# Linear attention into a tanh-shrink MLP: reordering the opening of batch 0 and moving work of batches 1 and 2 to later slots

## The chip, the cores and the metric

The kernel runs on one NeuronCore of one Trainium2 chip. The metric is the time of one execution on the device in microseconds (us); the median of three runs of the kernel before is 284.67 us (284.21 to 284.73). The engines are named as the profile names them: PE (TensorE matmuls), PEld (its weight loads), DVE (VectorE), ACT (ScalarE), POOL (GpSimd) and SP (the sync engine, which here only issues DMAs). Each engine takes its instructions strictly in the order in which they stand; an instruction that waits holds up everything behind it on its engine.

## The reference, cut to what matters

```python
def phi(x): return np.where(x > 0, x, np.exp(x) - 1.0) + 1.0      # = min(exp(x), max(x,0)+1)
q_p, k_p = phi(q), phi(k)                     # 8 batches, 8 heads, 576 tokens, 64 wide
kv  = einsum('bhsd,bhse->bhde', k_p, v)       # 64 x 64 for each head
z   = sum(k_p, axis=2)
num = einsum('bhsd,bhde->bhse', q_p, kv)
den = einsum('bhsd,bhd->bhs', q_p, z)[..., None] + 1e-06
x   = (num / den) -> [4608 tokens, 512]       # batch after batch
h   = x @ w_in                                # 512 -> 2048, "layer 1"
out = (h - tanh(h)) @ w_out                   # 2048 -> 512, "layer 2"
```

All inputs and the output are float32 in DRAM; the kernel turns them into bf16 as they are loaded.

## The kernel before, in words

**Two streams in one program.** The MLP runs over nine chunks `c` of 512 tokens. The attention runs over eight batches of 576 tokens and writes `xT`, the transposed input of layer 1. Batch 0 is computed before the MLP starts (the opening). The work of later batches is laid between the MLP's matmuls by hand: `s1[fi]` is a list of actions to be issued after layer 1's output block `fi` (16 blocks of 128 features, four matmuls of 128x512 each), and `s2[s]` one after slot `s` of layer 2 (16 slots of four matmuls). In chunk `c` the two streams work on batch `c+1` (denominator, numerator, scaling) and `c+2` (phi, kv, loads). The scheduling is manual: what the text of the kernel lists is the order on each engine, and nothing reorders it.

**Attention of a batch.** `phi_pieces` gives three actions for a half `i` of the heads: the exponential (ACT, tile `e`), `max(x,0)+1` (DVE, tile `r`) and the minimum of both (DVE, tile `qp` or `kp`). `a_kv`, `kv_cols_mm` and `b0_kv` make kv, which is copied from PSUM into `kz`; next to it `kz` holds the masked z. `qT` is the transposed phi(q): by PE transposes and two copies for each half in batches 0 and 1 (`a_qT_pe`), by one DMA transpose issued on SP from batch 2 on (`a_qT_dma`). `a_den` makes the denominators in one bank of PSUM and takes the reciprocal on DVE (`rden`, 128x144). The reciprocals are then brought to the layout of the numerators: for batch 0 and 1 by PE matmuls with a selection matrix (`b0_spread`, `a_spread_pe`), for batch 2 by DMA (`a_spread`): four small writes to DRAM (`ds`) and, once they have landed, two broadcast reads of 576 KB each (`rdb`). The numerators of batch 2 are then multiplied by `rdb` on DVE (`num_scale`, L401, four instructions of 128x512).

**The opening** on PE: 18 idle matmuls (`spin`), transposes of q, then z, kv, denominator and numerator of half 0 and 1 of the heads (`b0_z`, `b0_kv`, `a_den`, `b0_num`), the spread, and layer 1 of chunk 0, whose first four blocks are computed in halves of 256 tokens (L686), so that each of the eight scaling instructions (`b0_scale`, L304) releases four matmuls. The numerators are copied from PSUM to the tile `ns` by ACT (`b0_evac`, L293).

**PSUM** is one tile of eight banks, `ps_all`. Layer 1 of chunk 1 and later uses banks 0 to 5 in turn (`fi % 6`), so block `fi` can start only when DVE has read block `fi - 6` (the subtraction `gT`, L437, one instruction for two blocks, after ACT's tanh, L436).

**Loads.** q, k and v of a batch come by three DMAs issued on POOL. `qraw` and `kraw` have one buffer each. The loads of batch 3 stand on POOL behind `gate`, a copy of one element of `qT` of batch 2: they are issued only after the DMA transpose of batch 2 has landed. On SP the order at this place is: the DMA transpose of batch 2, the eight stores of chunk 0's output (held back in the list `later`), the four `ds` and two `rdb` transfers of batch 2, the stores of chunk 1.

Of the kernel before, what the change touches and what calls it, by code (L numbers as in the profile page):

```python
# [18 lines left out]
def kernel(  # L19
# [130 lines left out]
    def new_qT(b):  # L150
        qT_t[b] = work.tile([128, 2, J, 2, 64], BF16, name="qT")
# [4 lines left out]
            out=qT_t[b].rearrange("p i j g t -> p (i j) (g t)"),  # L156
            in_=qp_t[b].rearrange("p i j h d -> p (i j h d)"))

    def a_qT_pe(b, i, banks, on=None):
        if i == 0:  # L160
            new_qT(b)
        for n in range(2):
            j0, j1 = ((0, 5), (5, 9))[n]
            ps = banks().bitcast(BF16).rearrange("p (j t) -> p j t", t=128)
            for j in range(j0, j1):
                nc.tensor.transpose(ps[:, j - j0, :], qp_t[b][:, i, j].rearrange("p h d -> p (h d)"), ident)  # L166
            src = ps[:, 0:j1 - j0, :]
            dst = qT_t[b][:, i, j0:j1].rearrange("p j g t -> p j (g t)")
            if (on or "AV")[n] == "A":
                nc.scalar.copy(dst, src)  # L170
            else:
                nc.vector.tensor_copy(dst, src)

    def quads():

# [88 lines left out]
                                 v_b[0][rs, h, i, j, :], start=(j == 0), stop=(j == J - 1))  # L264

    def b0_kz(i):
        (nc.scalar.copy if i else nc.vector.tensor_copy)(kz_t[0][:, :, i, 0:64], ps_all[:, 2 * i:2 * i + 2, 0:64])

    def num_mm(b, i, bank_of):

# [14 lines left out]
    def b0_num(i):  # L285

        b0 = 2 * i
        num_mm(0, i, lambda h: b0 + h)
# [39 lines left out]
    def a_den(b, bank, parts=range(4)):  # L328

        kz, qT = kz_t[b], qT_t[b]  # L330
        ps = ps_all[:, bank, 0:J * 16]
        for t in range(4) if b == 0 else ():
            nc.tensor.matmul(ps[32 * t:32 * t + 32], eps[:, 0:32], one[:, 0:J * 16], start=True, stop=False)
        for n, p in enumerate((0, 2, 1, 3)):
            if n in parts:
                for t in range(4):
                    nc.tensor.matmul(ps[32 * t:32 * t + 32], kz[:, p // 2, p % 2, 64:96],  # L337
                                     qT[:, p % 2, :, p // 2, 16 * t:16 * t + 16],
                                     start=(n == 0 and b > 0), stop=(n == NP - 1))
        if b > 0:  # L340
            den = rpool.tile([128, J * 16], F32, name="den")
            nc.vector.tensor_scalar(den, ps, 1e-6, None, ALU.add)
        else:
            den = ps
        rden = rpool.tile([128, J * 16], F32, name="rden")
        nc.vector.reciprocal(rden, den)
        rden_t[b] = rden

    def a_split(b):
# [86 lines left out]
        nc.scalar.activation(th, h, AF.Tanh)  # L436
        nc.vector.tensor_sub(gT[:, fi:fi + 2, :], h, th)  # L437

    def l1act(fi, h, gT):
        th = mpool.tile([128, 2, 512], F32, name="th")[:, 0, :]  # L440
        nc.scalar.activation(th, h, AF.Tanh)  # L441
        nc.vector.tensor_sub(gT[:, fi, :], h, th)  # L442

    def gate(qT):

# [91 lines left out]
    for f in (eq0, rq0, mq0, eq1, rq1, mq1):  # L537
        f()
    spin(18)
    a_qT_pe(0, 0, side, "AV")  # L540
    (ek0, rk0, mk0), (ek1, rk1, mk1) = (phi_pieces(0, k_t, kp_t, "kp", i, 2 * i) for i in range(2))
    for f in (ek0, rk0):
        f()
    spin(5)
    a_qT_pe(0, 1, side, "AV")
    for f in (*ek1, mk0, rk1):
        f()
    spin(6)
    b0_z(0)
    spin(3)  # L550
    for f in mk1:
        f()
    b0_zc(0)
    b0_kv(0)
    b0_z(1)
    b0_zc(1)
    b0_kz(0)
    a_den(0, 4)
    ns0 = new_ns(0)
    spread_rest(0)  # L560
    b0_num(0)
    b0_kv(1)
    b0_kz(1)
    b0_evac(0, ns0)
    b0_num(1)
    b0_evac(1, ns0)
    b0_spread((0, 2, 1, 3), 0)
    for x in range(2):
        for n, p in enumerate((0, 2, 1, 3)):
            b0_scale(p, ns0, n, 4 * x, 4 * x + 4)  # L570

    def prepare():

# [12 lines left out]
    for c in range(NC):  # L586
# [4 lines left out]
        if c == 0:  # L591
            sub = {}

            def spread1():
                a_spread_pe(1, range(NP))
                for p in range(NP):
                    a_scale(1, p, sub["ns"], p)

            def kv1():
                a_kv(1, 4)  # L600
                pss = rest_mm(0, 4, 256)
                a_kz(1, 4)
                scale_rest(0, pss)

            def num1():
                ns = sub["ns"] = new_ns(1)
                for i in (1, 0):
                    b0 = 4 + 2 * i
                    num_mm(1, i, lambda h: b0 + h)
                    nc.scalar.copy(ns[:, i::2, 0:8, :].rearrange("p a j t -> p a (j t)"), ps_all[:, b0:b0 + 2, :])  # L610

            s2[0].append(lambda: a_qphi(1, 0))
            s2[1].append(lambda: a_qphi(1, 1))
            s2[4].append(lambda: a_kphi(1, 0))
            s2[5].append(lambda: (a_qT_pe(1, 0, Banks([4, 5])), a_qT_pe(1, 1, Banks([6, 7])), a_kphi(1, 1),
                                  load_q(2), load_k(2), load_v(2)))
            s2[2].append(prepare)
            s2[8].append(kv1)
            s2[9].append(lambda: (a_den(1, 4), num1(), spread_rest(1), a_split(1)))
            s2[12].append(spread1)  # L620

            qs, ks = [], []

            def exp2(pieces, src, store, name, i):
                pieces.append(phi_pieces(2, src, store, name, i))
                pieces[i][0]()

            def rest2(f):
                f[1]()
                f[2]()  # L630

            def k2(i):
                ks.append(phi_pieces(2, k_t, kp_t, "kp", i))
                ks[i][1]()

            s2[11].append(lambda: exp2(qs, q_t, qp_t, "qp", 0))
            s2[13].append(lambda: (rest2(qs[0]), exp2(qs, q_t, qp_t, "qp", 1)))
            s2[15].append(lambda: (rest2(qs[1]), a_qT_dma(2), [f() for f in later], k2(0), k2(1)))
        elif n1 < B:
            if c == 1:  # L640
                def kv2():
                    kv_cols_mm(2, 6, 0)
                    pss = rest_mm(1, 6, 256)
                    kz_copy(2, 6, 0)
                    scale_rest(1, pss)

                s1[8].append(kv2)
            if n1 < QS:
                s1[12].append(lambda: (a_den(n1, 6), a_spread(n1)))
            else:  # L650
                if c == 2:
                    s1[2].append(lambda: (q_den(n1, 0, 0), q_den(n1, 0, 1)))
                e = 2 * (c == 2)
                s1[3 + e].append(lambda: q_den(n1, 1, 0))
                s1[5 + e].append(lambda: q_den(n1, 1, 1))
                s1[7 + e].append(lambda: q_scale(n1))
            m = 12 if c == 1 else 9
            s2[m].append(lambda: a_num(n1, n2 if n2 < B else 0))
            if n2 < B:
                s2[m + 2].append(lambda: (q_zb(n2, 4 if c == 1 else 7), q_prod(n2)))  # L660
                if c > 1:
                    s2[15].append(lambda: (q_den(n2, 0, 0), q_den(n2, 0, 1)))
        if c == 1:
            for i in range(2):
                s1[1 + 2 * i].append(lambda i=i: (ks[i][0](), ks[i][2]()))
            s1[0].append(lambda: (a_vp(2, 0, nc.gpsimd), a_vp(2, 1, nc.gpsimd),
                                  gate(qT_t[n1]), load_k(n2), load_q(n2), load_v(n2)))
        if c >= 1 and n2 < B:
            d = 2
# [8 lines left out]
        if c == 0:  # L678

            first = Banks([4, 5, 6, 7, 0, 1, 2, 3])  # L680
            hs = [ps_all[:, n, :] for n in range(4)]
            for x in range(2):
                xs = slice(256 * x, 256 * x + 256)
                for n, p in enumerate((0, 2, 1, 3)):
                    for fi in range(4):
                        nc.tensor.matmul(hs[fi][:, xs], w_in_sb[:, p, fi * 128:(fi + 1) * 128], xT[:, p, xs],  # L686
                                         start=(x == 0 and n == 0), stop=(x == 1 and n == 3))
            for fi in range(4):
                l1act(fi, hs[fi], gT)
        for fi in range(4 if c == 0 else 0, NF):  # L690
            h = first() if c == 0 else ps_all[:, fi % 6, :]
            if c == 2 and fi == 1:

                for two in (0, 2):
                    for f, o in ((0, ps_all[:, 0, :]), (1, h)):
                        for p in (two, two + 1):
                            l1mm(c, f, o, p, p)
            elif c != 2 or fi > 1:
                for p in range(NP):
                    l1mm(c, fi, h, p, p)  # L700
            if c == 0:
                l1act(fi, h, gT)
            elif fi % 2:
                n = fi % 6
                l1act2(fi - 1, ps_all[:, n - 1:n + 1, :], gT)
            for f in s1[fi]:
                f()
# [56 lines left out]
```

## Time and profile before

| what | value |
|---|---|
| median of three runs | 284.67 us (284.21 to 284.73) |
| the profiled execution's own time | 284.32 us |
| its span, first to last instruction | 282.6 us |
| PE busy | 277.0 us, 98% of the span |
| DVE busy | 176.1 us, 62% |
| ACT busy | 145.6 us, 52% |
| POOL busy | 77.5 us, 27% |
| granted TensorE clock | 1.00 |
| first matmul of layer 1, chunk 0 (L686) | 16.82 us after the span's start |
| layer 1 of chunk 1 starts (L430) | 48.57 us |
| layer 1 of chunk 2 starts (L430) | 79.06 us |

The page gives busy time by engine, the span in 40 slices, the DMA queues, the chain of work that ended last and the costliest groups of instructions. A row of the timeline reads: start, duration, engine, source line, operation, output tile `<-` input tiles, shapes, count, and in brackets how long the engine had sat idle before it and what ended that. Starts are microseconds from the span's start. Durations of rows with a count above one reach from the first start to the last end. Line numbers are those of the kernel before.

### The profile page before, as it was taken

To read this page: it belongs to the slowest core of one execution; us is meant where nothing else is said; L and a number is where in the kernel's file an instruction comes from. 1 tells how busy PE (TensorE), PEld (TensorE's weight loads), DVE (VectorE), ACT (ScalarE), POOL (GpSimd) and SP (SyncE) were. 2 spreads that over 40 slices of the span, in tenths; PEclk is the share of its full clock that TensorE was granted. 3 is DMA by queue.
4 is the path that set the end of the run, shared out by engine and by line. 5 is a ranking of instruction groups with operands and counts; after the bars stand their busy time and mean duration, and the time that the engine had idled before them with its cause. 6 is when DMAs were issued, how large, how long until landed. Compare 5 with 4: busy or idle time off the path is not lost.

```text
span 282.6 us, 5093 instructions
## 1 busy us (share of the span) xinstructions
PE 277.0 (98%) x2084; PEld 131.9 (47%) x2084; DVE 176.1 (62%) x283; ACT 145.6 (52%) x176; POOL 77.5 (27%) x69
## 2 busy tenths in 40 slices
PE   8989999999999999999999999999999999999995
PEld 3564454454444454445444444444444444444443
DVE  5859977984779773977397639764870167006600
ACT  3648647946346753566366735572651365126411
POOL 8653120430361526233614360506050000000000
PEclk9999999999999999999999999999999999999999
DMA  6999999899994399049903792252115210230032
GB/s 103 199 207 212 205 207 209 172 192 197 236 237 76 71 194 217 5 84 162 220 22 73 115 240 60 48 110 48 29 22 123 58 32 2 57 79 13 2 74 75
DMA packets 38743, 33.12 MB, mean 117 GB/s; under 512 B 16160, under 2 KB 34624, under 8 KB 38592
## 3 DMA queue, kind: packets, MB, share of 16 engines
q0 software_dynamic: 17504, 18.35, 40.1%
q1 hardware_dynamic: 21216, 14.45, 21.8%
q8 instruction: 16, 0.26, 0.3%
q14 instruction: 7, 0.06, 0.1%
HBM read 38.14 MB, written 9.46 MB: 168 GB/s over the span
## 4 chain that ended last, share of the span: by engine, by line
PE 90%; DMA 5%; POOL 1%; ACT 1%; issue 1%; SPq 0%; DVE 0%; DVEq 0%; POOLq 0%
PE ps_all L430 43%; PE ps_all L451 41%; DMA v<-in_v_dram 3%; DMA out_dram<-osb 3%; PE ps_all L184 2%; PE ps_all L273 2%; PE ps_all L686 1%; ACT osb L462 1%; SPq L475 0%; POOL kraw L89 0%; PE ps_all L337 0%; POOL qraw L89 0%; PE ps_all L300 0%; PE ps_all L166 0%; PE ps_all L263 0%
## 5 line engine op out<-in xcount | busy, mean ns | idle before, releaser
L451 PE MATMUL ps_all<-w_out_sb,gT 128*128 128x512 bf16 x560 | 124.6, 379 | 0.0
L430 PE MATMUL ps_all<-xT,w_in_sb 128*128 128x512 bf16 x560 | 122.7, 379 | 0.0
L437 DVE TENSOR_TENSOR gT<-ps_all,th 128x1024 bf16<-128x1024 f32 x64 | 77.8, 1218 | 46.4 <-ACT th L436 46.4
L436 ACT ACTIVATE th<-ps_all 128x1024 f32<-128x1024 f32 x64 | 65.5, 1024 | 46.9 <-PE ps_all L430 46.9
L430 PEld LDWEIGHTS <-w_in_sb 128*128 128x128 bf16 x560 | 54.6, 98 | 65.5
L451 PEld LDWEIGHTS <-gT 128*128 128x128 bf16 x560 | 53.8, 98 | 63.2 <-issue 0.2
L462 ACT COPY osb<-ps_all 128x512 f32<-128x512 f32 (+1 forms) x36 | 20.7, 582 | 56.4 <-PE ps_all L451 40.0
L245 POOL TENSOR_TENSOR qp<-qp,rd 128x1152 bf16<-128x1152 bf16 x10 | 21.0, 2118 | 39.1 <-issue 23.7
L231 POOL TENSOR_TENSOR pr<-qp,zb 128x1152 f32<-128x1152 bf16 x10 | 23.5, 2362 | 21.6 <-ACT zb L224 21.6
L236 DVE TENSOR_REDUCE dn<-pr 128x9 f32<-128x576 f32 x20 | 14.5, 745 | 12.2 <-POOL pr L231 12.2
L136 ACT ACTIVATE e<-qraw 128x1152 bf16<-128x1152 bf16 x16 | 18.5, 1161 | 5.4 <-DMA qraw<-in_q_dram 5.4
L136 ACT ACTIVATE e<-kraw 128x1152 bf16<-128x1152 bf16 x15 | 17.4, 1162 | 1.9 <-DMA kraw<-in_k_dram 1.9
L138 DVE TENSOR_TENSOR qp<-e,r 128x1152 bf16<-128x1152 bf16 x16 | 12.1, 759 | 4.4 <-ACT e L136 3.3
L92 POOL DMA_DIRECT2D kraw<-in_k_dram x7 | 5.4, 769 | 33.1 <-DVE r L137 17.7
L138 DVE TENSOR_TENSOR kp<-e,r 128x1152 bf16<-128x1152 bf16 x15 | 11.4, 763 | 4.4 <-ACT e L136 3.5
L441 ACT ACTIVATE th<-ps_all 128x512 f32<-128x512 f32 x16 | 9.4, 597 | 5.5 <-PE ps_all L686 3.7
L442 DVE TENSOR_TENSOR gT<-ps_all,th 128x512 bf16<-128x512 f32 x16 | 10.4, 687 | 2.7 <-ACT th L441 1.7
L532 PE MATMUL ps_all<-zero 128*128 128x512 bf16 x32 | 10.1, 475 | 1.2 <-DVE zero L485 1.2
L92 POOL DMA_DIRECT2D qraw<-in_q_dram x7 | 5.2, 741 | 16.7 <-ACT e L136 7.3
L137 DVE TENSOR_SCALAR r<-qraw 128x1152 bf16<-128x1152 bf16 x16 | 7.4, 465 | 0.4 <-DMA qraw<-in_q_dram 0.4
L460 DVE COPY osb<-ps_all 128x128 f32<-128x128 f32 x1 | 0.3, 292 | 11.6 <-DMA out_dram<-osb 11.6
L199 DVE COPY vp<-v 128x1152 bf16<-128x1152 bf16 x10 | 5.3, 525 | 3.2 <-DMA v<-in_v_dram 3.2
(105 smaller groups left out, 141.1 us busy)
## 6 DMA issues: line engine op xcount, KB each, us to landing
out_dram<-osb SPq DMA_DIRECT2D x62, 128.0 KB, 2.5
qraw<-in_q_dram POOLq DMA_DIRECT2D x7, 576.0 KB, 10.5
kraw<-in_k_dram POOLq DMA_DIRECT2D x7, 576.0 KB, 7.8
v<-in_v_dram POOLq DMA_DIRECT2D x6, 576.0 KB, 11.4
w_in_sb<-in_moe_w_in_dram POOLq DMA_DIRECT2D x3, 512.0 KB, 13.1
w_out_sb<-in_moe_w_out_dram POOLq DMA_DIRECT2D x3, 512.0 KB, 16.3
v<-in_v_dram POOLq DMA_DIRECT2D x4, 288.0 KB, 12.9
rdb<-ds SPq DMA_DIRECT2D x2, 576.0 KB
```

The source lines that it names most:

```text
L92: nc.gpsimd.dma_start(out=t.rearrange("q h i j d -> q (h i) (j d)"), in_=x.rearrange("(n q) x -> q n x", n=4))
L136: return (lambda: nc.scalar.activation(e, x, AF.Exp), lambda: nc.vector.tensor_scalar(r, x, 0.0, 1.0, ALU.max, ALU.add), lambda: nc.vector ...
L138: lambda: nc.vector.tensor_tensor(y, e, r, ALU.min))
L231: nc.gpsimd.tensor_mul(pr_t[b][:, i].rearrange("p j h d -> p j (h d)"), qp_t[b][:, i].rearrange("p j h d -> p j (h d)"), zb_t[b][:, i].uns ...
L236: nc.vector.tensor_reduce(dn_t[b][:, i, :, h], pr_t[b][:, i, :, h, :], mybir.AxisListType.X, ALU.add)
L245: nc.gpsimd.tensor_mul(x, x, rd[:, i].unsqueeze(2).to_broadcast([128, J * 2, D]))
L430: nc.tensor.matmul(h, w_in_sb[:, p, fi * 128:(fi + 1) * 128], xT[:, p, c * 512:(c + 1) * 512], start=(n == 0), stop=(n == NP - 1))
L436: nc.scalar.activation(th, h, AF.Tanh)
L437: nc.vector.tensor_sub(gT[:, fi:fi + 2, :], h, th)
L442: nc.vector.tensor_sub(gT[:, fi, :], h, th)
L451: nc.tensor.matmul(o, gT[:, fi, i * 128:(i + 1) * 128], w_out_sb[:, fi, :], start=(fi == 0), stop=(fi == NF - 1))
L462: nc.scalar.copy(osb[:, f0:f1], o[:, f0:f1])
```

## The change

In the opening:

- the copies of `qT` become actions that the caller places; the DVE copy of half 1 stays first, the ACT copy (`t1a`) goes behind the two exponentials of k's second half;
- one `spin` matmul less at two places (5 to 4, 3 to 2);
- `kz` of half 0 is copied by ACT and `kz` of half 1 by DVE (the reverse of before);
- the reciprocal of batch 0 is two instructions, over columns 0 to 127 and 128 to 143;
- on PE the spread stands ahead of the numerator of half 1 (before: behind it), and the evacuation of half 0 ahead of kv of half 1;
- the eight scalings go by halves of the heads first (pairs 0, 2 for all tokens, then pairs 1, 3), and the first 32 matmuls of layer 1 are reordered to match; the four PSUM outputs are laid across two banks each.

In batches 1 and 2:

- chunk 0's layer 2: kv of batch 1 from slot 8 to 9, denominator and numerator from 9 to 10, spread and scaling from 12 to 13, the exponential of q of batch 2 (half 0) from 11 to 13; the exponential of half 1 leaves slot 13;
- chunk 1's layer 1 takes its blocks 0 and 1 in an interleaved order, as chunk 2 did already;
- phi(q) half 1 of batch 2, the DMA transpose of batch 2 and the held-back stores go from slot 15 of chunk 0 to behind block 1 of chunk 1 (only `max(x,0)+1` of that half stays in slot 15); phi(k) of batch 2 from behind blocks 1 and 3 to behind 3 and 5; kv of batch 2 from behind block 8 to 10; denominator and spread of batch 2 from behind block 12 to 13; the gate and the loads of batch 3 from behind block 0 to 1.

```diff
-    def a_qT_pe(b, i, banks, on=None):
+    def a_qT_pe(b, i, banks, on="AV"):
...
-            if (on or "AV")[n] == "A":
-                nc.scalar.copy(dst, src)
-            else:
-                nc.vector.tensor_copy(dst, src)
+            copies.append((nc.scalar.copy if on[n] == "A" else nc.vector.tensor_copy, dst, src))
+        return [lambda f=f, d=d, x=x: f(d, x) for f, d, x in copies]
...
-        (nc.scalar.copy if i else nc.vector.tensor_copy)(kz_t[0][:, :, i, 0:64], ps_all[:, 2 * i:2 * i + 2, 0:64])
+        (nc.vector.tensor_copy if i else nc.scalar.copy)(kz_t[0][:, :, i, 0:64], ps_all[:, 2 * i:2 * i + 2, 0:64])
...
-        nc.vector.reciprocal(rden, den)
+        for x in (slice(0, 128), slice(128, 144)) if b == 0 else (slice(0, 144),):
+            nc.vector.reciprocal(rden[:, x], den[:, x])
...
-    a_qT_pe(0, 0, side, "AV")
+    for f in a_qT_pe(0, 0, side):
+        f()
...
-    spin(5)
-    a_qT_pe(0, 1, side, "AV")
-    for f in (*ek1, mk0, rk1):
+    spin(4)
+    t1a, t1v = a_qT_pe(0, 1, side)
+    for f in (t1v, *ek1, t1a, mk0, rk1, *mk1):
         f()
     spin(6)
     b0_z(0)
-    spin(3)
-    for f in mk1:
-        f()
+    spin(2)
     b0_zc(0)
     b0_kv(0)
+    b0_kz(0)
     b0_z(1)
     b0_zc(1)
-    b0_kz(0)
     a_den(0, 4)
     ns0 = new_ns(0)
-    spread_rest(0)
     b0_num(0)
+    b0_evac(0, ns0)
     b0_kv(1)
     b0_kz(1)
-    b0_evac(0, ns0)
+    spread_rest(0)
+    b0_spread((0, 2, 1, 3), 0)
     b0_num(1)
     b0_evac(1, ns0)
-    b0_spread((0, 2, 1, 3), 0)
-    for x in range(2):
-        for n, p in enumerate((0, 2, 1, 3)):
-            b0_scale(p, ns0, n, 4 * x, 4 * x + 4)
+    for i in range(2):
+        for x in range(2):
+            for n, p in ((2 * i, i), (2 * i + 1, 2 + i)):
+                b0_scale(p, ns0, n, 4 * x, 4 * x + 4)
...
-            s2[8].append(kv1)
-            s2[9].append(lambda: (a_den(1, 4), num1(), spread_rest(1), a_split(1)))
-            s2[12].append(spread1)
+            s2[9].append(kv1)
+            s2[10].append(lambda: (a_den(1, 4), num1(), spread_rest(1), a_split(1)))
+            s2[13].append(spread1)
...
-            s2[11].append(lambda: exp2(qs, q_t, qp_t, "qp", 0))
-            s2[13].append(lambda: (rest2(qs[0]), exp2(qs, q_t, qp_t, "qp", 1)))
-            s2[15].append(lambda: (rest2(qs[1]), a_qT_dma(2), [f() for f in later], k2(0), k2(1)))
+            s2[13].append(lambda: exp2(qs, q_t, qp_t, "qp", 0))
+            def k2r():
+                qs.append(phi_pieces(2, q_t, qp_t, "qp", 1))
+                qs[1][1]()
+                for i in range(2):
+                    k2(i)
+
+            s2[15].append(lambda: (rest2(qs[0]), k2r()))
...
-                s1[8].append(kv2)
+                s1[10].append(kv2)
             if n1 < QS:
-                s1[12].append(lambda: (a_den(n1, 6), a_spread(n1)))
+                s1[13].append(lambda: (a_den(n1, 6), a_spread(n1)))
...
         if c == 1:
+            s1[1].append(lambda: (qs[1][0](), qs[1][2](), a_qT_dma(2), [f() for f in later]))
             for i in range(2):
-                s1[1 + 2 * i].append(lambda i=i: (ks[i][0](), ks[i][2]()))
-            s1[0].append(lambda: (a_vp(2, 0, nc.gpsimd), a_vp(2, 1, nc.gpsimd),
+                s1[3 + 2 * i].append(lambda i=i: (ks[i][0](), ks[i][2]()))
+            s1[1].append(lambda: (a_vp(2, 0, nc.gpsimd), a_vp(2, 1, nc.gpsimd),
                                   gate(qT_t[n1]), load_k(n2), load_q(n2), load_v(n2)))
...
-            hs = [ps_all[:, n, :] for n in range(4)]
-            for x in range(2):
-                xs = slice(256 * x, 256 * x + 256)
-                for n, p in enumerate((0, 2, 1, 3)):
-                    for fi in range(4):
-                        nc.tensor.matmul(hs[fi][:, xs], w_in_sb[:, p, fi * 128:(fi + 1) * 128], xT[:, p, xs],
-                                         start=(x == 0 and n == 0), stop=(x == 1 and n == 3))
+            hs = [ps_all[:, fi // 2:4:2, 256 * (fi % 2):256 * (fi % 2) + 256] for fi in range(4)]
+            for i in range(2):
+                for x in range(2):
+                    xs = slice(256 * x, 256 * x + 256)
+                    for f0 in (0, 2):
+                        for p in (i, i + 2):
+                            for fi in (f0, f0 + 1):
+                                nc.tensor.matmul(hs[fi][:, x, :], w_in_sb[:, p, fi * 128:(fi + 1) * 128], xT[:, p, xs],
+                                                 start=(p == 0 and fi == f0), stop=(p == 3 and fi > f0))
             for fi in range(4):
-                l1act(fi, hs[fi], gT)
+                l1act(fi, hs[fi], gT, 2)
...
-            if c == 2 and fi == 1:
+            if c in (1, 2) and fi == 1:
...
-            elif c != 2 or fi > 1:
+            elif c not in (1, 2) or fi > 1:
```

More of the change, by code (lines that the diff above doesn't have):

```diff
@@ L157, in a_qT_dma @@
             in_=qp_t[b].rearrange("p i j h d -> p (i j h d)"))
-    def a_qT_pe(b, i, banks, on=None):
+    def a_qT_pe(b, i, banks, on="AV"):
         if i == 0:
             new_qT(b)
+        copies = []
         for n in range(2):
@@ L437, in l1act2, with l1act @@
         nc.vector.tensor_sub(gT[:, fi:fi + 2, :], h, th)
-    def l1act(fi, h, gT):
-        th = mpool.tile([128, 2, 512], F32, name="th")[:, 0, :]
+    def l1act(fi, h, gT, x=0):
+        th, g = mpool.tile([128, 2, 512], F32, name="th")[:, 0, :], gT[:, fi, :]
+        if x:
+            th, g = (y.rearrange("p (x t) -> p x t", x=x) for y in (th, g))
         nc.scalar.activation(th, h, AF.Tanh)
-        nc.vector.tensor_sub(gT[:, fi, :], h, th)
+        nc.vector.tensor_sub(g, h, th)
     def gate(qT):
@@ L614 @@
             s2[4].append(lambda: a_kphi(1, 0))
-            s2[5].append(lambda: (a_qT_pe(1, 0, Banks([4, 5])), a_qT_pe(1, 1, Banks([6, 7])), a_kphi(1, 1),
+            s2[5].append(lambda: ([f() for i in range(2) for f in a_qT_pe(1, i, Banks([4 + 2 * i, 5 + 2 * i]))], a_kphi(1, 1),
                                   load_q(2), load_k(2), load_v(2)))
             s2[2].append(prepare)
-            s2[8].append(kv1)
-            s2[9].append(lambda: (a_den(1, 4), num1(), spread_rest(1), a_split(1)))
-            s2[12].append(spread1)
+            s2[9].append(kv1)
+            s2[10].append(lambda: (a_den(1, 4), num1(), spread_rest(1), a_split(1)))
+            s2[13].append(spread1)
             qs, ks = [], []
```

## The prediction, made before the result was known

> **What bounds the kernel.** I read the page first: PE is busy for 277.0 of 282.6 us, the granted clock is 1.00. Next the list of waits, restricted to PE:
>
> ```profile
> PE ps_all L532 <- DVE zero L485: 1.2, 1, 1.2
> PE ps_all L686 <- DVE xT L304: 0.6, 1, 0.6
> PE ps_all L273 <- ACT kz L267: 0.4, 1, 0.4
> ```
>
> These are all the waits of PE that stand out, and all lie before 16.82 us. After that PE streams: a 128x512 matmul starts every 0.216 us (48 of L430 take 10.36 us in the chain of waits). So the change can win in the opening only, and every new wait of PE later is lost time in full. Third, the timeline of the opening:
>
> ```profile
> 13.73 1.06 DVE L346 RECIPROCAL rden<-ps_all 128x144 f32<-128x144 f32 x1 [0.22 <-PE ps_all L337]
> ...
> 14.37 0.27 ACT L267 CAST kz<-ps_all 128x128 bf16<-128x128 f32 x1 [2.24 <-PE ps_all L263]
> ...
> 14.69 0.41 PE L273 MATMUL ps_all<-qT,kz 64*64 64x512 bf16 x4 [0.38 <-ACT kz L267]
> 15.03 1.17 PE L300 MATMUL ps_all<-rden,sel 32*128 32x128 f32 x32
> ...
> 16.34 2.74 DVE L304 TENSOR_TENSOR xT<-ns,ps_all 128x256 bf16<-128x256 f32 x8 [1.55 <-PE ps_all L300]
> ...
> 16.82 3.65 PE L686 MATMUL ps_all<-xT,w_in_sb 128*128 128x256 bf16 x32 [0.61 <-DVE xT L304]
> ```
>
> The reciprocal ends at 14.79, but the spread starts at 15.03: it stands behind the numerator of half 1, which waited for ACT's kz. Last, the timelines of ACT, DVE, SP, POOL and PE from 50 to 80 us, where the second part of the change acts:
>
> ```profile
> 50.49 1.02 ACT L436 ACTIVATE th<-ps_all 128x1024 f32<-128x1024 f32 x1
> ...
> 51.18 2.83 SPq L155 DMA_TRANSPOSE qT<-qp  x1
> 54.12 5.63 SPq L475 DMA_DIRECT2D out_dram<-osb  x8
> ...
> 55.91 0.18 POOL L447 COPY g<-qT 1x1 bf16<-1x1 bf16 x1 [1.15 <-DMA qT<-qp]
> 56.48 0.74 POOL L92 DMA_DIRECT2D kraw<-in_k_dram  x1 [0.40 <-issue]
> ...
> 57.95 0.76 POOL L92 DMA_DIRECT2D v<-in_v_dram  x1
> ...
> 68.75 1.12 SPq L369 DMA_DIRECT2D rdb<-ds  x2
> ...
> 70.67 0.46 DVE L199 COPY vp<-v 128x1152 bf16<-128x1152 bf16 x1 [3.17 <-DMA v<-in_v_dram]
> ...
> 76.62 0.42 DVE L212 CAST zr<-ps_all 128x256 bf16<-128x256 f32 x1 [1.13 <-PE ps_all L184]
> 76.96 0.41 DVE L214 CAST kz<-ps_all 128x256 bf16<-128x256 f32 x1
> 77.29 2.48 DVE L401 TENSOR_TENSOR xT<-ps_all,rdb 128x512 bf16<-128x512 f32 x4
> ...
> 79.06 2.11 PE L430 MATMUL ps_all<-xT,w_in_sb 128*128 128x512 bf16 x9
> ```
>
> The reader is to see a chain of transfers: DMA transpose of batch 2, gate, loads of batch 3, v landing at 70.6, DVE waiting 3.17 us for it, and close behind it the scaling L401 and chunk 2. The fourth L401 ends at 79.77 (released at 79.83); PE wants it for the sixth matmul of chunk 2, at 79.06 + 5 x 0.216 = 80.14. **The slack is 0.31 us.** By the trace's landing marks the two rdb transfers landed at 74.5 and 77.1, the second 0.2 before L401 started.
>
> **The change, part by part. Opening.** The chain up to the reciprocal's start (13.73) begins with the landing of k's second half (10.8: ACT sat idle 0.43 us for it) and is not shortened. The spin matmul removed in each of two places (0.216 each) lies ahead of waits for k and v (PE stood still for 0.15 before kv at 12.25, and z waits for DVE): 0. The copy t1a (0.68) now starts behind the two exponentials, about 12.05, and ends at 12.75; PE needs it at 13.37: 0. ACT's kz of half 0 then ends at about 13.05, before 13.6 when PE wants it: 0. The evacuation of half 0 starts at 14.1 instead of 14.5, not needed before 16: 0.
>
> The reciprocal in two pieces: 128x144 took 1.06, a 128x36 one (L242) 0.38, so 6.3 ns for a column and 0.15 fixed; 0.96 and 0.25, with the 0.08 by which neighbours on DVE overlap: 1.13, ending at 14.86. In the built order only the second piece signals, so the spread waits for both and starts at 14.92: 0.11 earlier, not 0.29. Bounds: 14.74 if the first piece alone released it, 15.05 if a piece pays 0.15 more. [...]
>
> The spread (1.17, idle PE may save 0.1 of its start) ends at 16.0 to 16.1, the first scaling starts 0.14 later as before, at 16.18. The new matmul order needs the second scaling after two matmuls instead of four: the scaling's pitch is 0.33, two matmuls 0.22, so 0.11 is lost. Layer 1's 32 matmuls end at 20.25 instead of 20.29. The numerator of half 1 runs under the first scaling and its evacuation (1.02) ends at about 17.45; the fifth scaling wants it at 17.50 and PE's second token half at 17.64: hidden with 0.05 to 0.2 to spare. **Opening: -0.05** (between -0.29 and +0.10). I take the value by the signal that the program has.
>
> **Batch 1, slots 9, 10, 13.** The same instructions relative to PE, one slot (0.86) later; DVE's phi(k), which ended 0.25 before PE used it, gains cover: 0. But the scaling of batch 1 (L423, 2.48 us) now has two slots before layer 1 of chunk 1, not three: its fourth ends 3.01 after the spread's first matmul, PE reaches chunk 1 after 2.07. The interleaved blocks 0 and 1 put the fourth pair at position six, 2.07 + 1.08 = 3.15 with 3.07 needed: 0, cover 0.08; without it the rest of a matmul pair, at most 0.3.
>
> **Batch 2, the term that decides.** On ACT the exponential of q's half 1 stands behind the tanh of blocks 0 and 1, which PE releases at about 50.4. Tanh 50.44 to 51.46, exponential (1.16) to 52.53. On DVE its minimum stands behind the subtraction of blocks 0 and 1 (51.8 to 53.0) and ends at 53.7; before it ended at 51.11. So SP issues the DMA transpose at 53.76 instead of 51.18: **2.58 later**. Behind it on SP the eight stores move to 56.7, on POOL the gate to 58.5 and the three loads to 59.1 to 60.5. PE's own use of qT, the denominator of batch 2, has 3 us of cover. On DVE the subtractions are held up by phi's minima (0.76 each), but blocks 8 and 10 find their banks free with 0.5 and 0.4 left: 0. The denominator moves behind block 13 (+0.6) and on DVE behind the subtraction of blocks 12 and 13: the ds writes go from 63.68 to 65.3 (+1.6). They took 3.9 us to land, so rdb is issued at about 70.5 instead of 68.75.
>
> Are the loads just shifted? From 56 to 68 the DMA engines ran at shares of 0.92 to 1.22, full; from 52 to 54.5 there is now nothing to move, and that time is lost. v lands at 73.1 instead of 70.55. DVE's queue from vp to L401 is 6.62 long less 1.13 of idle time: L401 not before 73.25 + 5.49 = 78.7. The other input, rdb, landed 8.3 after its issue: 78.85 if it only shifts with its issue (+1.75), 79.7 if it shifts with the loads it queues with (+2.58). L401 starts between 78.7 and 79.7 instead of 77.29; PE waits for the shift less 0.31 less the 0.05 by which it is early: 1.05 to 2.05. I take the middle, 79.2, since from 62 to 66 loads and SP's transfers moved side by side: **+1.55**. [...]
>
> **Sum**: 284.32 (profiled execution; span 282.6 and 1.7 around it) - 0.05 + 1.55 = 285.8. The median of the runs is 0.35 above that execution; with half of it, 286.0.
>
> **Rivals.** *The late transfers stay hidden* (not slower): the DMA engines were at a share of 0.74 from 68 to 70 and 0.63 from 50 to 52, so late loads might catch up. It decides if v lands by 72.1 (1.5 late) and rdb by 77.4. For it: the idle 1.13 on DVE. Against: rdb landed 0.2 before use, and the transpose is 2.58 late by engine order alone. Time 284.3 to 284.6. *The opening gives its full worth and nothing is lost later*: spread at 14.74, layer 1 0.29 earlier, and the 0.25 for which PE waits inside the numerator of batch 1 (behind DVE's den, L342) gone too: 283.8. Against it: the signal of the second piece, and that wait's order is kept. *A second wait*: the covers of 0.08 at chunk 1's start and 0.4 at block 10 fall as well, with L401 at 79.7 or later: 2.05 + 0.3 + 0.4 more, 287 and above.
>
> **Chances.** Forecast 0.64, with its own range 285.1 (opening -0.29, wait 1.05) to 286.8 (+0.10, 2.05, median's 0.35); hidden 0.18; full opening 0.08; second wait 0.10. About 0.2% (0.57 us) is what a measurement here can tell from no change; the forecast and the second wait lie beyond it, hidden within it, the full opening beyond it on the other side. From 284.4 to 286.9 the range leaves out the full opening and the second wait.
>
> **What would show it.** In the profile after: the spread behind two reciprocals at about 14.9 and L1's first matmul near 16.65; the DMA transpose issued near 53.8; the gate near 58.5; DVE's vp waiting for v until about 73; a wait of PE for DVE's xT (L401's successor) at the start of chunk 2, 1 to 2 us, the first in PE's list after the opening. I am wrong if that wait is missing: then the loads or rdb landed earlier than the shift says, or phi(q) half 1 came sooner than 53.

## The result and the profile after

The changed kernel takes 287.01 us (median of six runs, 286.55 to 289.98) against 284.27 for the kernel before in the same comparison (six runs, 284.05 to 284.73): a ratio of 1.0109, 95% interval 1.0067 to 1.0151. It is slower, by 2.7 us; the forecast was 286.0 with a range from 284.4 to 286.9. The profiled execution took 286.92 us with a span of 285.2 (before 284.32 and 282.6), so 2.60 us are to be found between the two traces. Single executions of kernels whose loads of batch 3 come late were now and then 3 to 8 us longer (289.98 here), at a mean granted clock of 0.988 to 0.994; the medians hardly feel them, but the profiled execution of e1 below is one.

Most line numbers have moved by one or two, the first matmuls of layer 1 by more: what was L686 is L696; L441/L442 (tanh and subtraction of chunk 0) are L443/L444, and L304 (first scaling) is L303. "PE loses" means below: by so much two of its matmuls start further apart than they do without a wait. The first lines of the list of PE's waits (engine and line that waited, for whom; us in total, how often, the longest):

```profile
PE ps_all L430 <- DVE xT L401: 1.3, 3, 0.9
PE ps_all L534 <- DVE zero L487: 1.2, 1, 1.2
PE ps_all L430 <- DVE gT L444: 0.8, 1, 0.8
```

Two waits of layer 1 are new. The first line is the one that was forecast; the third was not. The timeline of the opening and of chunk 0's layer 1 shows where the third comes from:

```profile
13.62 1.07 DVE L346 RECIPROCAL rden<-ps_all 128x128 f32<-128x128 f32 x2 [0.42 <-PE ps_all L336]
...
14.75 1.17 PE L299 MATMUL ps_all<-rden,sel 32*128 32x128 f32 x32 [0.53 <-DVE rden L346]
...
16.06 2.74 DVE L303 TENSOR_TENSOR xT<-ns,ps_all 128x256 bf16<-128x256 f32 x8 [1.22 <-PE ps_all L299]
...
16.53 3.77 PE L696 MATMUL ps_all<-xT,w_in_sb 128*128 128x256 bf16 x32 [0.27 <-DVE xT L303]
...
20.53 0.69 DVE L444 TENSOR_TENSOR gT<-ps_all,th 128x512 bf16<-128x512 f32 x1 [1.73 <-ACT th L443]
21.25 0.60 ACT L443 ACTIVATE th<-ps_all 128x512 f32<-128x512 f32 x1 [0.76 <-DVE gT L444]
21.88 0.69 DVE L444 TENSOR_TENSOR gT<-ps_all,th 128x512 bf16<-128x512 f32 x1 [0.66 <-ACT th L443]
22.67 0.60 ACT L443 ACTIVATE th<-ps_all 128x512 f32<-128x512 f32 x1 [0.82 <-DVE gT L444]
...
25.40 6.20 PE L430 MATMUL ps_all<-xT,w_in_sb 128*128 128x512 bf16 x28 [0.78 <-DVE gT L444]
```

Up to the matmuls of L696 this is the opening as forecast: spread right behind two reciprocals, first scaling, first matmul. From the start of the reciprocal to the first matmul of L430 it takes 6.52 us instead of 6.57. Below it, ACT and DVE take turns: each of these tanhs waits for the subtraction of the block before it, and each subtraction for its tanh. One block takes 1.35 to 1.42 us. In the kernel before, a pair of tanhs followed the next at 1.41, 0.71 a block:

```profile
20.18 1.09 ACT L441 ACTIVATE th<-ps_all 128x512 f32<-128x512 f32 x2 [3.71 <-PE ps_all L686]
21.59 1.20 ACT L441 ACTIVATE th<-ps_all 128x512 f32<-128x512 f32 x2 [0.33 <-DVE gT L442]
```

Block 9 is written to bank 1. In the changed kernel this bank holds the first 256 tokens of blocks 2 and 3, so four subtractions must end first; before, it held block 1 alone, and two were enough. The fourth subtraction ends at 25.34, and PE, which wanted the bank at 24.45, stands still (a matmul that follows at 0.216 otherwise follows at 1.16: 0.945 lost). Layer 1 of chunk 0 from first L430 to layer 2 takes 11.30 instead of 10.36.

The timeline from 50 to 82 us, the second part of the change:

```profile
54.49 2.85 SPq L155 DMA_TRANSPOSE qT<-qp  x1
57.45 6.00 SPq L477 DMA_DIRECT2D out_dram<-osb  x8
59.22 0.18 POOL L449 COPY g<-qT 1x1 bf16<-1x1 bf16 x1 [3.80 <-DMA qT<-qp]
59.80 0.74 POOL L92 DMA_DIRECT2D kraw<-in_k_dram  x1 [0.40 <-DVE gT L437]
...
66.26 1.30 SPq L366 DMA_DIRECT2D ds<-rden  x4
71.60 1.12 SPq L369 DMA_DIRECT2D rdb<-ds  x2
73.15 0.46 DVE L198 COPY vp<-v 128x1152 bf16<-128x1152 bf16 x1 [4.61 <-DMA v<-in_v_dram]
80.21 1.89 DVE L401 TENSOR_TENSOR xT<-ps_all,rdb 128x512 bf16<-128x512 f32 x3 [1.58 <-DMA rdb<-ds]
80.96 0.38 PE L430 MATMUL ps_all<-xT,w_in_sb 128*128 128x512 bf16 x1 [0.88 <-DVE xT L401]
```

Chunk 1 starts at 49.34 instead of 48.57, so 0.77 of every start here is handed down from above. v lands and DVE goes through its queue, but then it sits idle for 1.58 us before L401, and what ends that is rdb, not v. By the starts of single matmuls PE loses 1.05 + 0.38 + 0.33 = 1.76 us at chunk 2's start.

The sum: 0.94 (banks) + 1.76 (chunk 2) - 0.05 (opening) - 0.11 (k's second half landed that much earlier in this execution) = 2.54 of the 2.60.

### The profile page after: what moved, and what is told of

It is laid out like the page before. It is cut to its first block, busy times and chain, and to the rows that moved or that the text cites. A ratio compares the mean times of both kernels' runs of the same rounds, so it can differ in the third digit from the quotient of the medians.

```text
span 285.2 us, 5089 instructions
## 1 busy us (share of the span) xinstructions
PE 276.9 (97%) x2082; PEld 131.4 (46%) x2082; DVE 175.8 (62%) x284; ACT 146.3 (51%) x176; POOL 77.6 (27%) x69
## 4 chain that ended last, share of the span: by engine, by line
PE 82%; DMA 9%; DVE 3%; ACT 1%; POOL 1%; SPq 1%; issue 1%; DVEq 0%; ACTq 0%; POOLq 0%
PE ps_all L430 41%; PE ps_all L453 35%; DMA rdb<-ds 3%; DMA v<-in_v_dram 3%; DMA out_dram<-osb 2%; PE ps_all L183 2%; DMA ds<-rden 2%; PE ps_all L696 1%; PE ps_all L272 1%; DVE gT L444 1%; DVE xT L401 1%; ACT th L443 1%; DVE rden L346 1%; ACT osb L464 1%; SPq L477 0%
## 5 line engine op out<-in xcount | busy, mean ns | idle before, releaser
L430 PE MATMUL ps_all<-xT,w_in_sb 128*128 128x512 bf16 x560 | 123.2, 379 | 2.1 <-DVE xT L401 1.3
L430 PEld LDWEIGHTS <-w_in_sb 128*128 128x128 bf16 x560 | 54.7, 98 | 68.2 <-issue 3.2
L244 POOL TENSOR_TENSOR qp<-qp,rd 128x1152 bf16<-128x1152 bf16 x10 | 21.0, 2118 | 40.8 <-issue 23.7
L444 DVE TENSOR_TENSOR gT<-ps_all,th 128x512 bf16<-128x512 f32 x16 | 10.5, 688 | 4.5 <-ACT th L443 3.8
L443 ACT ACTIVATE th<-ps_all 128x512 f32<-128x512 f32 x16 | 9.4, 597 | 6.3 <-DVE gT L444 3.8
L534 PE MATMUL ps_all<-zero 128*128 128x512 bf16 x30 | 9.0, 453 | 1.2 <-DVE zero L487 1.2
```

The lines of the kernel that those rows point to most:

```text
L244: nc.gpsimd.tensor_mul(x, x, rd[:, i].unsqueeze(2).to_broadcast([128, J * 2, D]))
L430: nc.tensor.matmul(h, w_in_sb[:, p, fi * 128:(fi + 1) * 128], xT[:, p, c * 512:(c + 1) * 512], start=(n == 0), stop=(n == NP - 1))
L444: nc.vector.tensor_sub(g, h, th)
```

## The experiments

Three questions were open: whether the shared banks are all of the first stall (e1, e9, e4), how the two halves of the change add up (e2, e3), and which of the moved items makes rdb late: the DMA transpose with the loads behind it, the mass of transfers, or the denominator's own slot (e5 to e8, e10). The kernel before had medians of 284.37 beside e1 to e4, 284.42 beside e5 to e8, and 284.73 beside e9 and e10.

**e1: the changed kernel, tanh and subtraction bank by bank.** The matmuls and their banks stay; ACT and DVE take one bank (two blocks, 256 tokens) at a time.

```diff
-            for fi in range(4):
-                l1act(fi, hs[fi], gT, 2)
+            for x in range(2):
+                for f0 in (0, 2):
+                    h = ps_all[:, 2 * x + f0 // 2, :]
+                    th = mpool.tile([128, 2, 512], F32, name="th")[:, 0, :]
+                    nc.scalar.activation(th, h, AF.Tanh)
+                    nc.vector.tensor_sub(gT[:, f0:f0 + 2, 256 * x:256 * x + 256],
+                                         h.rearrange("p (f t) -> p f t", f=2), th.rearrange("p (f t) -> p f t", f=2))
```

> The changed kernel, with one thing mended: the tanh and the subtraction of chunk 0's first four blocks go bank by bank (each instruction covers two blocks for 256 tokens, so that ACT and DVE never share a bank) instead of block by block across two banks. Theory A (the 0.78 us wait of PE for gT at 25.4 us comes from ACT's tanh waiting for DVE's subtraction on the shared banks): tanh of the first four follow each other every 0.7 us again, that wait is gone, 0.8 to 0.95 us off the whole: 286.1 us; the wait for rdb at chunk 2's start stays at 1.3 to 1.8. Rival (PE waits because block 9 now needs four subtractions instead of two, whatever their pace): the wait stays, 287.0 us.

Measured: 286.42 (286.09 to 289.33), ratio 1.0096 (1.0059 to 1.0132). The wait for the subtraction is gone: from the first L430 to layer 2 it takes 10.36 again. But the execution that was profiled was the longest of the four, 289.33: the transfer of v of batch 3 was on the chip with its first of 16 parts at 72.3 and with its last at 76.85, and PE waited 3.0 us in two pieces for v's projection. Right behind these waits, from 79.98 on, the granted clock was 0.50 for 3.41 us, and 128x512 matmuls started 0.427 apart instead of 0.216. So this trace shows the opening, not chunk 2.

**e9: the same kernel again**, for an undisturbed profile.

> The kernel of e1 once more, for a profile in which no transfer is held up. If the tanh and the subtraction of the first four blocks, taken bank by bank, give back only the stall at block 9, the profiled execution is 286.0 to 286.3 us, the wait for v's projection (2.98 us in e1) is gone, and the waits for xT of batch 2's spread at chunk 2's start lose 1.3 to 1.9 us, as in the changed kernel (1.76). If the wait for v's projection belongs to this order of the opening rather than to a late transfer, it is there again with some 3 us, and the time is 288 or more.

Measured: 286.14 (285.5 to 286.4), ratio 1.0052 (1.0035 to 1.0068). The first line of its list of waits, and ACT in chunk 0:

```profile
PE ps_all L430 <- DVE xT L401: 1.5, 3, 1.1
```

```profile
19.12 1.08 ACT L702 ACTIVATE th<-ps_all 128x512 f32<-128x512 f32 x2 [1.70 <-PE ps_all L696]
20.53 1.19 ACT L702 ACTIVATE th<-ps_all 128x512 f32<-128x512 f32 x2 [0.33 <-DVE gT L703]
```

Two tanhs stand in one row again, 1.41 a pair, and the wait for v's projection has not come back: it was the late transfer, not this order. The stall at chunk 2 is 1.25 + 0.38 + 0.34 = 1.97 us, a little above the expected 1.9. So the shared banks, read block by block, cost the changed kernel 0.945 us of PE, of which 0.2 is taken back at chunk 2; spans 285.2 and 284.4. By the medians, each against the kernel before of its own comparison, the changed kernel lies 2.74 above, this one 2.05 (e1) and 1.41 (e9).

This edit changes two things: the pace (0.71 instead of 1.4 us a block), and that bank 1 is free after the second subtraction instead of the fourth. The pace alone would do: in e9 even the fourth subtraction ends at 22.45, and block 9 starts at 24.55. So the rival, four subtractions whatever their pace, is refuted. By estimate the count alone would do as well: in the changed kernel the second subtraction ended at 22.57. It took both to make the wait.

**e2: the opening alone**, with the slots of batches 1 and 2 as before.

```diff
-            s2[9].append(kv1)
+            s2[8].append(kv1)
...
-                s1[13].append(lambda: (a_den(n1, 6), a_spread(n1)))
+                s1[12].append(lambda: (a_den(n1, 6), a_spread(n1)))
```

> The opening of the changed kernel with the slots of batches 1 and 2 of the kernel before. If the late DMA transpose is the larger half of the loss: no wait of PE at chunk 2's start, the wait for gT in chunk 0 (0.8 to 0.95) stays, the opening's gain is 0.05 to 0.2: 284.9 to 285.2 us. If the wait at chunk 2 is only the consequence of chunk 0's wait: it stays too, 286.5 us or more.

Measured: 286.0 (285.53 to 287.02), ratio 1.0063 (1.0045 to 1.0081). From its list of waits:

```profile
PE ps_all L430 <- DVE gT L437: 1.0, 1, 1.0
PE ps_all L430 <- DVE gT L444: 0.8, 1, 0.8
...
PE ps_all L183 <- DVE kp L138: 0.5, 1, 0.5
```

The opening alone is slower, and the bank stall does not stay alone. PE loses 0.95 us by it, but DVE falls back further: its last phi(k) of batch 1 starts at 40.66 instead of 39.00, 1.66 late. With kv of batch 1 in slot 8 PE meets it (0.62 us lost at 40.8); in the changed kernel, with the same DVE time of 40.66, kv stands in slot 9 and there is no such wait. The third wait, 1.18 us behind 54.97, follows a slow stretch on DVE: two of its instructions that make `r` for k took 1.40 us each (52.46 and 53.78) while POOL's two copies `vp<-v` ran, from 52.07 to 54.87; before, they took 0.45 each and were done at 51.84, ahead of POOL's copies (51.99). The subtraction that PE wants stands behind them on DVE and starts at 55.10. (The profiled execution was the longest of the four, so these three are not the median's loss.)

**e3: the slots alone**, with the opening as before.

```diff
-            hs = [ps_all[:, fi // 2:4:2, 256 * (fi % 2):256 * (fi % 2) + 256] for fi in range(4)]
+            hs = [ps_all[:, n, :] for n in range(4)]
...
-    spread_rest(0)
-    b0_spread((0, 2, 1, 3), 0)
     b0_num(1)
     b0_evac(1, ns0)
+    b0_spread((0, 2, 1, 3), 0)
```

> The opening of the kernel before with the slots of batches 1 and 2 of the changed kernel. If the late transfers cost by themselves: DMA transpose issued at 53.7, rdb landing at about 79.3, L401 at about 79.4, PE waits 1.3 to 1.9: 285.6 to 286.2 us. If they matter only together with the opening: 284.3 us.

Measured: 286.12 (285.77 to 286.29), ratio 1.0061 (1.0048 to 1.0073). PE loses 0.99 + 0.38 + 0.33 = 1.70 us at chunk 2's start, and another 0.30 behind 77.67, ahead of a small matmul; no other wait of the MLP is new. The slots cost 1.75 us by themselves.

**e4: the opening alone, with e1's order of tanh and subtraction.**

> The opening of the changed kernel with the bank-by-bank tanh and the slots of before: the opening's own worth. By the timeline of the changed kernel (first matmul of layer 1's next blocks at 20.14 instead of 20.30, of which 0.11 is an earlier landing of k): 0.05 to 0.2 us faster than the kernel before, 284.1 us, no wait of PE at chunk 2. If putting the spread ahead is worth nothing: 284.3.

Measured: 284.30 (283.7 to 285.19, twelve runs), ratio 0.9998 (0.9985 to 1.0011). Not to be told from before. The opening is 0.05 to 0.06 us shorter (6.51 from reciprocal to L430). In this execution the reciprocal also started 0.41 earlier than in the profile before, and two waits of 0.24 and 0.18 us, at 39.6 and 49.9, take both back: they lie behind exponentials for which ACT waited for the loads of k and q, and which started at 35.60 and 46.57 (before: 35.45 and 46.38). In this execution, what the opening gained was lost where the loads came no earlier. Beside e2 it says that all of the opening's loss is the bank order; beside e1, of the same comparison, that the slots cost 2.1 us, and with e9, each against its own kernel before, 1.5.

**e5: e1's kernel with the DMA transpose early again.** phi(q) half 1, the transpose and the held-back stores are back in slot 15 of chunk 0; everything else of batch 2 stays late, the denominator behind block 13.

```diff
-            s2[15].append(lambda: (rest2(qs[0]), k2r()))
+            s2[15].append(lambda: (rest2(qs[0]), exp2(qs, q_t, qp_t, "qp", 1), rest2(qs[1]),
+                                   a_qT_dma(2), [f() for f in later], k2(0), k2(1)))
...
-            s1[1].append(lambda: (qs[1][0](), qs[1][2](), a_qT_dma(2), [f() for f in later]))
```

> The changed kernel with the bank-by-bank tanh, and phi(q) half 1, the DMA transpose and the held-back stores of batch 2 back in slot 15 of chunk 0 (exponential there too); all other slots as changed, the denominator of batch 2 behind block 13 among them. Theory B (the transfers of batch 3 and 2 are late because the DMA transpose is issued 2.6 us later): transpose issued near 52, v of batch 3 landing near 71.4; rdb still issued about 1.6 late because of the denominator: L401 near 78.3 to 78.8 instead of 79.3 or more, 284.7 to 285.2 us. Rival (the denominator's slot alone makes rdb late): rdb and L401 as with the late transpose, 286.1.

Measured: 285.66 (285.26 to 286.31, ten runs), ratio 1.0041 (1.0029 to 1.0053). SP and DVE from 50 to 82 us:

```profile
51.88 2.88 SPq L155 DMA_TRANSPOSE qT<-qp  x1
...
65.33 1.29 SPq L366 DMA_DIRECT2D ds<-rden  x4
70.47 1.12 SPq L369 DMA_DIRECT2D rdb<-ds  x2
71.37 0.46 DVE L198 COPY vp<-v 128x1152 bf16<-128x1152 bf16 x1 [3.77 <-DMA v<-in_v_dram]
78.86 2.48 DVE L401 TENSOR_TENSOR xT<-ps_all,rdb 128x512 bf16<-128x512 f32 x4 [1.56 <-DMA rdb<-ds]
```

The transpose is 2 us earlier, v lands at 71.25 (before 70.55, e9 72.59), and still L401 waits for rdb: PE loses 1.33 us. For this wait the late transpose isn't needed.

**e6: e5 with denominator and spread of batch 2 back behind block 12.**

```diff
-                s1[13].append(lambda: (a_den(n1, 6), a_spread(n1)))
+                s1[12].append(lambda: (a_den(n1, 6), a_spread(n1)))
```

> As the early transpose, and the denominator and spread of batch 2 back behind block 12. Theory B with both causes of rdb's lateness gone: rdb issued near 69, landing near 77.5, no wait of PE at chunk 2 or at most 0.3: 284.0 to 284.4 us. If the moved slots cost something that is not yet named: 284.8 or more.

Measured: 284.35 (283.81 to 285.19, eleven runs), ratio 0.9993 (0.998 to 1.0005). The same view:

```profile
63.72 1.29 SPq L366 DMA_DIRECT2D ds<-rden  x4
68.75 1.12 SPq L369 DMA_DIRECT2D rdb<-ds  x2
...
77.34 2.48 DVE L401 TENSOR_TENSOR xT<-ps_all,rdb 128x512 bf16<-128x512 f32 x4
```

One slot of one action, and L401 starts with no idle time ahead of it; PE has no wait at chunk 2. With e4 this is the best of the versions with the new opening, and like e4 it is no faster than the kernel before.

**e7: e1's kernel with the denominator behind block 12, the transpose late.** The edit of e6 on e1.

> The changed kernel with the bank-by-bank tanh and only the denominator and spread of batch 2 back behind block 12: rdb is issued near 69.5 instead of 71, the loads of batch 3 stay late. If rdb lands with its own issue: L401 is then held by v's chain, near 78.6, 285.4 to 285.7 us. If rdb queues behind the loads: L401 unchanged, 286.1 us.

Measured: 285.71 (284.71 to 293.5, ten runs), ratio 1.0051 (1.0025 to 1.0078). In the profiled execution (284.71) PE loses 0.65 us at chunk 2, and it is v's chain that sets it: vp at 72.69, DVE's queue of 5.4 us behind it, L401 at 78.09 without idle time, rdb on the chip at 77.91.

```profile
72.69 0.46 DVE L198 COPY vp<-v 128x1152 bf16<-128x1152 bf16 x1 [4.98 <-DMA v<-in_v_dram]
...
78.09 2.48 DVE L401 TENSOR_TENSOR xT<-ps_all,rdb 128x512 bf16<-128x512 f32 x4
```

But this execution is the shortest of the ten, and the median lies a whole us above it. So by the median the late transpose alone costs 1.29 us, as much as the late denominator alone in e5 (1.24). That v's load varies from run to run and here has no cover left would explain the difference; no trace of a longer execution of this kernel shows it.

**e8: e1's kernel without the eight held-back stores of chunk 0.**

```diff
-            s1[1].append(lambda: (qs[1][0](), qs[1][2](), a_qT_dma(2), [f() for f in later]))
+            s1[1].append(lambda: (qs[1][0](), qs[1][2](), a_qT_dma(2)))
```

> The changed kernel with the bank-by-bank tanh; the eight held-back stores of chunk 0's output (1 MB) are left out, so the first 512 tokens of the output are not written. The DMA transpose stays late. If what makes rdb and v late is the volume that the DMA engines must move between the transpose and chunk 2: about 5 us of transfers are gone, v lands near 70, rdb near 76, the wait at chunk 2 vanishes: 284.2 to 284.5 us. If it is the order of issue alone: v lands near 73, 286 us.

Measured: 285.57 (285.27 to 286.16, eight runs), ratio 1.0039 (1.0025 to 1.0052). With 1 MB less to move (eight stores of 128 KB) v lands at 70.44, as early as before, though the transpose is late (53.48). rdb, however, is issued at 70.47 and landed at 78.85, to 0.1 us as in e5, and PE loses 1.31 us. Beside e9, leaving out this 1 MB moves v's landing by 2.15 us (72.59 in e9), rdb's issue by 0.46 us (70.93 in e9), and rdb's time from issue to landing not at all (8.38, in e9 8.41).

**e10: e5 with the denominator behind block 14.**

> As e5, but with the denominator and the spread of batch 2 behind block 14 instead of block 13. Theory that the slot behind a block sets the denominator: one block is about 0.8 us, so the two transfers of the reciprocal are issued and land 0.6 to 0.9 us later than in e5 (the second is on the chip at 79.4 to 79.6 instead of 78.76), and the time is 286.2 to 286.6. Theory that VectorE's order sets it (in both kernels the reciprocal stands right behind the subtraction of blocks 12 and 13, whatever TensorE does ahead of it): issue and landing as in e5 within 0.2 us, and 285.6 to 285.8.

Measured: 285.57 (285.26 to 286.31), ratio 1.0039 (1.0023 to 1.0054). ds is issued at 65.12, rdb at 70.17, and the second one is on the chip at 78.43. This execution's reciprocal of batch 0 started 0.20 earlier than e5's (13.43 against 13.63), and so did everything behind it: counted from there ds is issued at the same time to 0.01 us. In both kernels DVE takes the denominator right behind the subtraction of blocks 12 and 13; a block more of cover on PE is not seen. It is the place in DVE's queue that counts.

Four kernels with e1's opening make a table, in us: what PE loses at the start of chunk 2 in the profiled execution, and in brackets the median less that of the kernel before beside it:

| | transpose early | transpose late |
|---|---|---|
| denominator behind block 12 | 0 (-0.07, e6) | 0.65 (1.29, e7) |
| denominator behind block 13 | 1.33 (1.24, e5) | 1.97 (1.41, e9; 2.05, e1) |

Each move alone costs 1.2 to 1.3 us by the median, and both together cost less than the sum: L401 waits for the later of two chains, rdb's and v's.

## Why the prediction was wrong, and where it was right

**The opening: what was costed was right, and a term was missing.** The spread starts 1.13 us behind the start of the reciprocal; 1.19 was taken. It took 1.17 us, after 0.53 of idle time on PE, and 1.17 before, without idle time; that an idle PE saves up to 0.1 of its start is shown by no run. From reciprocal to L430 0.05 was to be gained, and 0.05 was. That part's walk ended with "Layer 1's 32 matmuls end at 20.25 instead of 20.29", and this is the step that failed: it stopped at the matmuls. The diff lays each of the four outputs across two banks, two blocks to a bank, and the sentence on the matmul order says nothing of who reads these banks. The program has ACT's tanh wait for DVE's subtraction of the block before it. The row is plain: the subtraction of block 0 from 20.53 for 0.69, the tanh of block 1, in the same banks, at 21.25, 0.03 after its end; block 2, in the two other banks, waits too, and starts 0.10 after the subtraction of block 1. In e9, with the same matmuls and banks and one bank to an instruction, the pairs of tanhs follow at 1.41 again, and PE does not wait at block 9. Why the program has the wait is not shown, and no run here shows what would happen without it. Size: 0.945 us, forecast 0. Put into the forecast's own sum for the profiled execution, 285.8 + 0.945 makes 286.8, beside 286.92 measured. The 0.18 that the forecast added for the median did not show: beside the changed kernel the median of before was 284.27, not above its profiled execution (284.32). The wait could have been found before the run, in the signals of the built program, as that of the reciprocal's second piece was. Of the rival *a second wait* the time came true (287 and above), by a mechanism that it did not name: the covers of 0.08 at chunk 1's start and 0.4 at block 10 held.

**Batch 1, slots 9, 10, 13: 0, right.** From layer 2 of chunk 0 to chunk 1 it takes 17.90 us instead of 17.91. e2 shows that, with the bank stall there, the later slots even save the 0.62 that kv would wait.

**Batch 2: the size was right, what decides it was not.** In order, with the 0.77 that the opening handed down taken off: transpose issued at 53.72 (53.76 forecast), gate 58.45 (58.5), loads from 59.03 (59.1), ds 65.49 (65.3), rdb issued 70.83 (70.5), L401 79.44 (79.2). v landed at 73.03, 72.26 with the same correction (73.1 forecast); in e3, e7 and e9, which have no bank stall, at 72.85, 72.57 and 72.59. That is 2.0 to 2.3 later than before, not 2.55: the loads made up a little of their late issue. PE's wait of 1.76 lies between 1.05 and 2.05, 0.2 above the value taken; e3, with the opening of before, has 1.70.

The step that failed here is the upper end of the range for L401: rdb was to land either 8.3 us after its issue or as much later as the loads, "if it shifts with the loads it queues with", and the middle was taken. rdb shifts with its issue alone. From issue to its second landing it took 8.34 us before, 8.52 after, 8.45 in e3, 8.64 in e4, 8.29 in e5, 8.46 in e7, 8.38 in e8, 8.26 in e10, with the loads early or late and the stores early, late or left out; only in e1's disturbed execution it took 8.9. So in the changed kernel the chain that ends last is denominator, ds, rdb, L401, and it begins with the small edit from block 12 to 13, which puts the denominator on DVE behind one subtraction more: it starts at 63.91 in e5 and at 62.31 in e6, 1.6 late. The forecast had this 1.6. That the middle, 79.2, came so near to 79.44 is luck: the upper end did not hold, and the lower one, 78.85, was passed because rdb was issued 0.33 later than forecast and took 0.18 longer to land.

The late transpose is the second cause, by two ways, and by the medians not a smaller one (e7 beside e5). v's own chain gives L401 at about 78.1 in e7's profiled execution. And it pushes the eight stores to where ds is written: from the issue of ds to that of rdb it took 5.34 us after, 5.67 in e3, 5.66 in e9 and 6.10 in e7, but 5.03 to 5.24 where the stores came early or not at all (before, e2, e4, e5, e6, e8, e10). That rdb's issue moves with the stores is measured; that ds queues behind their packets is only argued.

**The rivals.** *Hidden*: refuted; it needed rdb by 77.4, and it came at 80.12 (79.35 without the 0.77). *The opening gives its full worth*: refuted; the spread waits for the second piece of the reciprocal (it starts at 14.75, 0.06 after that piece's end).

## What to carry to other kernels

When an output is laid out anew in PSUM, follow its readers as well as its writers: here four blocks laid across banks, two to a bank, and read block by block had ACT and DVE take turns (1.4 instead of 0.7 us a block), and the price, 0.945 us, fell on the matmul that wanted the bank back, six blocks later. When several things move at once, follow every chain that ends at the same instruction: here a 0.3 us instruction ahead of two DMAs in a row (5 and 8.4 us), moved by 1.6 us, cost by itself, in the medians, as much as 2.7 MB of late transfers did (1.24 and 1.29), and taking back one of the two left the other's price. And an item moved by one slot on PE may move by a whole queue entry on another engine, as here from block 12 to 13 (1.6 us), or, as from block 13 to 14, by none (0.01 us).

## What the runs showed of the hardware

- DVE's 284 instructions and ACT's 175 started, in the profile after, in the order in which the program has them; while DVE waited 4.61 us for v, ahead of `vp`, none of those behind it started.
- The reciprocal in two pieces took 1.07 us, in one piece 1.06; the second piece, 128x16, started 0.08 before the first one's end, so the split cost 0.01 instead of the 0.07 taken.
- The two rdb reads (576 KB each) took 8.3 to 8.6 us from the first issue to the second landing (8.9 in e1's disturbed execution), 8.4 both with 1 MB of stores ahead of them (e9) and without (e8).
- One transfer arrived in pieces far apart: the 16 parts of v of batch 3 landed in e1 from 72.3 to 76.85, where in e9 all were there at 72.6.
- In that execution of e1 PE stood still twice, 3.0 us together, between 75.75 and 79.38; from 79.98 to 83.39 the granted clock was 0.50, and eight steps of 0.427 instead of 0.216 us cost another 1.7. That the waits brought the clock down is not shown.
- DVE's `max(x,0)+1` on 128x1152 bf16 took 0.45 us, but 1.40 us while POOL copied `vp<-v` of the same size (e2). Why is not shown.
